# Plain block products in the first batch's first layer, a shorter range step, and the tokens' shares applied at each expert's drain

## Chip, core and metric

One core of one Trainium2 chip (trn2). The metric is the device time of one execution in microseconds (us), lower is better. TensorE (PE) multiplies, with its weight loads shown apart as PEld; VectorE (DVE), ScalarE (ACT) and GpSimd (POOL) do the elementwise work; SyncE's queue (SP) issues the transfers. PSUM holds eight banks of 128 x 512 float32 for products.

## What is computed

```python
def reference(q, k, v, centroids, w_in, w_out, w_gate, w1, w2):
    x = clustered_attention(q, k, v, centroids)   # B=2, H=8, S=768, D=64 -> x (1536, 512)
    h = x @ w_in                                  # w_in (512, 2048), held as float64
    g = np.maximum(h, 0.0) + np.log1p(np.exp(-np.abs(h)))
    x = g @ w_out                                 # MoE1; w_out (2048, 512), float64
    logits = x @ w_gate                           # (1536, 8)
    P = np.exp(logits - logits.max())
    for _ in range(8):
        P /= P.sum(1, keepdims=True) + 1e-09
        P /= P.sum(0, keepdims=True) + 1e-09
        P *= N / E
    for e in range(8):                            # MoE2: 8 experts, w1[e] (512, 1024), w2[e] (1024, 512)
        out += P[:, e:e + 1] * (np.maximum(x @ w1[e], 0.0) @ w2[e])
```

## The kernel before

Every product is taken with float32 operands split into a high and a low part, as three matmuls (high x high, high x low, low x high). The attention comes first: its steps stand in a list of events sorted by step number, and it leaves x transposed in `xt[sb]`, one tile for each of the 2 batches of 768 tokens.

The two MoE layers then run as 80 **units** (kind, batch, expert, fc): 2 x 8 units of MoE1 (kind 1) and 2 x 8 x 4 units of MoE2 (kind 2). A unit takes 256 hidden columns of one batch. Its **first layer** is `group(u, i)` (L649) for i = 0 to 6: seven block products of a Winograd-like 2 x 2 scheme, 6 matmuls of 384 columns each, 42 in all, accumulated in the PSUM banks la, lb and mb (mb shares la's or lb's bank by its tag). The scheme needs sums of blocks of x (`x_sums`, S1 to S4) and of the weights (`sums_`, T1 to T4, L215 on POOL), so the weight is split into seven slots `wh`, `wl` (L224 on ACT; L225 on POOL for kind 1, on DVE for kind 2); `w2_` splits the second weight (L230 on ACT, L231 on POOL). Banks are drained by copies c (L687) and DVE additions (L691, L695, L699), which leave the hidden values in `gf`. `act` (L706) applies softplus (Abs, Exp, Ln on ACT; a max-and-add on DVE, L720) or relu times the token's share `PB` (L727 on DVE), and `act_split` splits the result into `gh` (ACT cast, L733) and `gl` (DVE subtraction, L734). The **second layer** `layer2(u, part)` follows one unit later, in four parts between the groups of the next unit: kind 1, 24 pairs of matmuls of 512 and 256 columns (L753); kind 2, 36 matmuls of 512 columns (L772), summed over all experts in six banks y0 to y5, which are copied out at the end of a batch (L777).

`to32` (L114) turns the float64 words of w_in and w_out into float32, for batch 0's units alone (four halves of 128 x 512 a unit); batch 1 reads them back from a DRAM scratch. A half takes an Abs on ACT (L121) and on DVE a shift-and-mask (L122), two steps that join sign and low word (L123, L124) and the range step (L125), which zeroes what is too small.

In front of MoE2, `gate` and eight `sinkhorn` rounds make the shares `Pt`, from a queue of steps popped between groups. Five units (`NHOLD`) meanwhile run first layers only; then their drains (the list `late`) multiply by the shares, and their second layers follow. `spread_p` and `load_p` bring each expert's shares, spread over the partitions, from DRAM (`pb`). `GB` is the number of `gf` buffers. The program text gives a scheduler its order; each engine's instructions stand in the order that it chose.

Of the kernel before, what the change touches and what calls it, by code (L numbers as in the profile page):

```python
# [7 lines left out]
F32 = mybir.dt.float32  # L8
F32R = mybir.dt.float32r
# [11 lines left out]
def attention_moe_moe2(ctx, tc, q, k, v, centroids, w_in, w_out, w_gate, w1, w2, eye, out, dbg=None):  # L21
# [30 lines left out]
    GB = 2 * NF2 + 1  # L52
    NHOLD = 5
# [30 lines left out]

    first_blk = x_blocks(xt[0])

    def x_first(name):
        if name in SUMS:
            t = slot_pool["ap"].tile([P, KC // 2, S // 2], F32, tag="xs", name=f"xs{name}", bufs=2)
            x_sum(first_blk, name, t, nc.gpsimd)  # L90
        else:
            x_split("1_0", first_blk, int(name))

    def x_split(key, blk, i):
        name = COMBOS[i]
# [9 lines left out]
        XC[name] = hi, lo  # L105

# [7 lines left out]
    def to32(dst, raw, nm):  # L114
# [90 lines left out]
    def split_unit(u):  # L205
# [27 lines left out]
        return [sums_] + [lambda c=c: w1_(*c) for c in ((0, 2), (2, 4), (4, 7))], [lambda c=c: w2_(c) for c in range(2)]  # L233
# [383 lines left out]
    for n, x in enumerate(("S1", "S2", "3", "S4", "2", "5", "S3", "4", "0", "1", "6")):  # L617
        at(175 + n * 2, lambda x=x: x_first(x), ("xs", 0))
# [30 lines left out]
    def group(u, i):  # L649
# [54 lines left out]
    late = []  # L704

    def act(u, q, cols, ps=None):  # L706
# [4 lines left out]
        if kind == 1:  # L711
            if ps is not None:
# [25 lines left out]
    def layer2(u, part):  # L738
# [231 lines left out]
```

## Time and profile before

| | |
|---|---|
| median of 3 runs | 1684.97 us (1682.76 to 1688.23) |
| the profiled execution | 1685.95 us; span 1684.1 us |
| PE busy | 1581.2 us, 94% of the span, 8302 matmuls |
| DVE busy | 1181.9 us, 70% |
| ACT busy | 881.1 us, 52% |
| POOL busy | 776.9 us, 46% |
| granted PE clock, mean | 0.979 of full speed |

The profile is of one execution. Its span runs from the first to the last instruction; the device time has 1.85 us around it. "Busy" on DVE and POOL includes the time in which an instruction has started and is kept waiting. In a timeline each row is one instruction or a run of like ones, with its start, its length, its line, what it writes from what, its shape, how often, and in brackets the idle time of its engine before it with what ended that. Rows of a line give the shortest, the median and the longest duration in ns.

### The profile page before, as it was taken

The page shows a single profiled execution, that of the slowest core. Times are in us where ns is not written, and L with a number is a line of the kernel's source. Part 1 is how long each engine was busy: PE and PEld are TensorE (multiplying, and loading weights), DVE is VectorE, ACT ScalarE, POOL GpSimd, SP SyncE. Part 2 cuts the span into 40 slices and gives each one's busy share as a digit, 9 for nine tenths or more (in the row PEclk, how much of TensorE's full clock was granted, in tenths as well). Part 3 has the DMA queues.
Part 4 walks back from the last instruction along what each step waited for, and adds up shares of the span by engine and source line. Part 5 has one row for each costly group of instructions (what it writes and reads, how often), then busy time and mean ns, then how long its engine had stood idle before and what let it go on. Part 6 is the DMA issues. An engine that isn't in the chain of part 4 may idle for free.

```text
span 1684.1 us, 22932 instructions
## 1 busy us (share of the span) xinstructions
PE 1581.2 (94%) x8302; PEld 1404.1 (83%) x8302; DVE 1181.9 (70%) x1862; ACT 881.1 (52%) x1809; POOL 776.9 (46%) x741
## 2 busy tenths in 40 slices
PE   5899998877789998999999999999999999999999
PEld 4777887767678786889999999988999999999998
DVE  7999899899985466865655665668655555655653
ACT  5888887666667675434434433434434434433442
POOL 6444545156577665343444444445343343434441
PEclk8999999889989999999999999999999999999999
DMA  6232220044411211122122122222232122133221
GB/s 189 77 103 53 57 53 15 1 150 150 150 63 51 76 51 63 53 81 80 55 85 85 57 78 85 60 76 75 98 85 79 56 85 83 58 79 84 58 68 50
DMA packets 126017, 128.66 MB, mean 76 GB/s; under 512 B 7664, under 2 KB 99280, under 8 KB 125904
## 3 DMA queue, kind: packets, MB, share of 16 engines
q1 hardware_dynamic: 125760, 127.14, 25.2%
q8 instruction: 65, 1.06, 0.3%
q14 instruction: 48, 0.39, 0.1%
q10 hardware_dynamic: 144, 0.07, 0.0%
HBM read 107.72 MB, written 11.58 MB: 71 GB/s over the span
## 4 chain that ended last, share of the span: by engine, by line
PE 73%; DVE 17%; ACT 6%; issue 3%; POOL 1%; DMA 0%; SPq 0%; DVEq 0%; ACTq 0%
PE Y L772 30%; PE la L668 16%; PE mb L668 8%; PE lb L668 4%; PE av L571 3%; PE t L556 3%; PE s L525 3%; DVE gf L720 2%; PE y L753 2%; DVE gl L734 2%; DVE w2f L124 1%; DVE el L563 1%; DVE wl L225 1%; DVE w2f L123 1%; ACT E L538 1%
## 5 line engine op out<-in xcount | busy, mean ns | idle before, releaser
L215 POOL TENSOR_TENSOR wf<-wf 128x256 f32<-128x256 f32 x320 | 278.5, 889 | 394.2 <-DMA wf<-in_moe_w_dram 301.2
L733 ACT CAST gh<-gf 128x384 fp32r<-128x384 f32 x316 | 161.6, 513 | 490.2 <-DVE gf L727 445.5
L231 POOL TENSOR_TENSOR w2l<-w2f,w2h 128x512 fp32r<-128x512 f32 x160 | 251.5, 1592 | 320.6 <-ACT w2h L230 320.4
L772 PE MATMUL Y<-w2h,gh 128*128 128x512 f32 x768 | 299.0, 389 | 0.8 <-ACT gh L733 0.8
L772 PE MATMUL Y<-w2l,gh 128*128 128x512 f32 x768 | 298.9, 389 | 0.0
L772 PE MATMUL Y<-w2h,gl 128*128 128x512 f32 x768 | 298.5, 389 | 0.0
L734 DVE TENSOR_TENSOR gl<-gf,gh 128x384 fp32r<-128x384 f32 x316 | 224.8, 715 | 92.0 <-ACT gh L733 85.2
L695 DVE TENSOR_TENSOR gf<-la,c 128x384 f32<-128x384 f32 x79 | 43.9, 556 | 251.4 <-PE la L668 250.9
L224 ACT CAST wh<-wf 128x512 fp32r<-128x512 f32 (+1 forms) x240 | 159.2, 688 | 31.3 <-PE la L668 15.6
L772 PEld LDWEIGHTS Y<-w2h,gl 128*128 128x128 f32 x768 | 144.1, 188 | 29.9
L727 DVE SCALAR_TENSOR_TENSOR gf<-gf,pb 128x384 f32<-128x384 f32 x177 | 164.8, 932 | 4.0
L772 PEld LDWEIGHTS Y<-w2h,gh 128*128 128x128 f32 x768 | 144.0, 187 | 22.4 <-ACT gh L733 1.2
L772 PEld LDWEIGHTS Y<-w2l,gh 128*128 128x128 f32 x768 | 144.2, 188 | 21.2
L225 DVE TENSOR_TENSOR wl<-wf,wh 128x512 fp32r<-128x512 f32 (+1 forms) x195 | 150.6, 798 | 0.9 <-ACT wh L224 0.9
L668 PE MATMUL la<-chA,wh 128*128 128x384 f32 x320 | 110.7, 346 | 25.8 <-DVE gf L695 13.6
L668 PE MATMUL mb<-chS,wh 128*128 128x384 f32 x320 | 110.3, 345 | 8.9 <-DVE gf L691 8.8
L668 PE MATMUL la<-chA,wl 128*128 128x384 f32 x320 | 109.6, 342 | 3.6 <-POOL wl L225 3.6
L556 PE MATMUL t<-idf,E 128*128 128x128 f32 x576 | 100.5, 284 | 12.9 <-DVE el L563 7.3
L563 DVE TENSOR_TENSOR el<-t,eh 128x384 fp32r<-128x384 f32 x192 | 102.2, 546 | 11.9 <-ACT eh L559 9.8
L668 PE MATMUL la<-chS,wh 128*128 128x384 f32 x320 | 110.0, 344 | 0.2 <-ACT c L687 0.2
L668 PE MATMUL la<-clS,wh 128*128 128x384 f32 x320 | 109.4, 342 | 0.0
L668 PE MATMUL la<-chS,wl 128*128 128x384 f32 x320 | 109.3, 342 | 0.0
(204 smaller groups left out, 3574.6 us busy)
## 6 DMA issues: line engine op xcount, KB each, us to landing
wf<-in_moe_w_dram SPq DMA_DIRECT2D x128, 256.0 KB, 3.4
w2f<-in_moe_w_dram SPq DMA_DIRECT2D x128, 256.0 KB, 3.0
r<-in_moe_w_in_dram SPq DMA_DIRECT2D x16, 512.0 KB, 5.1
r<-in_moe_w_out_dram SPq DMA_DIRECT2D x16, 512.0 KB, 4.1
Bt<-AT SPq DMA_DIRECT2D x32, 192.0 KB, 2.5
pb<-pdram SPq DMA_DIRECT2D x15, 384.0 KB, 6.9
w<-wf SPq DMA_DIRECT2D x8, 512.0 KB, 4.3
w<-w2f SPq DMA_DIRECT2D x8, 512.0 KB, 4.2
```

Source lines behind the costliest of these rows:

```text
L215: nc.gpsimd.tensor_tensor(wf[:, SLOT[o_], :], wf[:, SLOT[u_], :], wf[:, SLOT[v_], :], ALU.subtract)
L224: nc.scalar.copy(wh[:, c0:c1], wf[:, c0 + 1 : c1 + 1, :])
L225: (nc.vector if kind == 2 or u == (1, 0, 0, 0) else nc.gpsimd).tensor_tensor(wl[:, c0:c1], wf[:, c0 + 1 : c1 + 1, :], wh[:, c0:c1].bitcast ...
L231: nc.gpsimd.tensor_tensor(w2l[:, c], w2v[:, c], w2h[:, c].bitcast(F32), ALU.subtract)
L525: nc.tensor.matmul(ps[:, kk, 0:CB], X[0, j][:, c : c + P], X[1, j][:, kk * CB : (kk + 1) * CB], start=m == 0, stop=m == 1,)
L556: nc.tensor.transpose(pt[:, t * P : (t + 1) * P], Et[i, t][:, s * P : (s + 1) * P], idf)
L563: nc.vector.tensor_tensor(el, TT.pop((i, s)), EHL[i, s].bitcast(F32), ALU.subtract)
L668: nc.tensor.matmul(ps, wt[:, s_, ks], xx[:, k_, :], start=i in (0, 1, 3) and n == 0, stop=n == 3 * nk - 1, skip_group_check=True,)
L727: nc.vector.scalar_tensor_tensor(g, src, 0.0, PB[sb, e][:, cols], ALU.max, ALU.mult)
L733: nc.scalar.copy(gh[:, cols], g)
L734: nc.vector.tensor_tensor(gl[:, cols], g, gh[:, cols].bitcast(F32), ALU.subtract)
L772: nc.tensor.matmul(y[m], gt[:, ms], wt[:, q, :], start=first and i == 0, stop=last and i == 2)
```

## The change

First, units of MoE1's first batch take plain 2 x 2 block products: `plain_group` (L703 in the changed file), four groups of 12 matmuls (48), which read the four blocks of x and of the weight themselves. Their weight has four slots, split in two pieces; the sums T1 to T4 and the x sums of that batch go, and the drains read PSUM directly. Second, `to32`'s range step becomes a maximum on the Abs result, from which the shift-and-mask then reads: on DVE two one-input and two two-input steps in place of one and three. Third, the relu of MoE2 writes `gh` (ACT) and `gl` (DVE) without the share; Y is drained after each expert by DVE as share times Y plus the sum so far (in `xt[sb]`'s memory), and `load_p`, `spread_p` and `late` go. Three units are held, with seven queue steps a unit; `gf` has 6 buffers, `gh` and `gl` 6 in place of 4.

```diff
-    GB = 2 * NF2 + 1
-    NHOLD = 5
+    GB = 6
+    NHOLD = 3
...
-        m = wp.tile([P, raw.shape[1]], F32, tag="cm", name="cm" + nm, bufs=1)
+        m = wp.tile([P, raw.shape[1]], I32, tag="cm", name="cm" + nm, bufs=1)
         d = dst.bitcast(I32)
-        nc.scalar.activation(m, H.bitcast(F32), AF.Abs)
-        nc.vector.tensor_scalar(d, H, 3, 0x3FFFFFFF, ALU.logical_shift_left, ALU.bitwise_and)
+        nc.scalar.activation(m.bitcast(F32), H.bitcast(F32), AF.Abs)
+        nc.vector.tensor_scalar(m.bitcast(F32), m.bitcast(F32), 2.0 ** -15, None, ALU.max)
+        nc.vector.tensor_scalar(d, m, 3, 0x3FFFFFFF, ALU.logical_shift_left, ALU.bitwise_and)
         nc.vector.scalar_tensor_tensor(d, H, -0x40000000, d, ALU.bitwise_and, ALU.bitwise_or)
         nc.vector.scalar_tensor_tensor(d, L, 29, d, ALU.logical_shift_right, ALU.bitwise_or)
-        nc.vector.scalar_tensor_tensor(dst, m, 2.0 ** -15, dst, ALU.is_ge, ALU.mult)
...
+        if is_plain(u):
+            return [lambda c=c: w1_(*c) for c in ((2, 4), (0, 2))], w2s
...
-    for n, x in enumerate(("S1", "S2", "3", "S4", "2", "5", "S3", "4", "0", "1", "6")):
-        at(175 + n * 2, lambda x=x: x_first(x), ("xs", 0))
+    for n in range(4):
+        at(175 + n * 5, lambda n=n: x_split("1_0", first_blk, n), ("xs", 0))
...
+    def plain_group(u, i):
...
+        q, half = i % 2, i // 2
+        ps = ps_l.tile([P, FH], F32, tag="l" + "ab"[q], name=f"p{i}" + nm)
+        nk, n = KC // 2, 0
+        for j in range(2):
+            hi, lo = XC[f"A{half + 1}{j + 1}"]
+            s_ = SLOT[f"B{j + 1}{q + 1}"]
+            for k_ in range(nk):
+                ks = slice(k_ * P, (k_ + 1) * P)
+                for wt, xx in ((wh, hi), (wh, lo), (wl, hi)):
+                    nc.tensor.matmul(ps, wt[:, s_, ks], xx[:, k_, :], start=n == 0, stop=n == 6 * nk - 1)
+                    n += 1
...
+        act(u, q, slice(half * FH, (half + 1) * FH), ps)
...
-            if ps is not None:
+            if ps is not None and not is_plain(u):
                 with tc.high_priority(40):
                     nc.scalar.copy(g, ps)
                 src = g
...
-        elif u in units[len(m1) : len(m1) + NHOLD]:
-            if ps is not None:
-                nc.scalar.copy(g, ps)
-            late.append((u, q, cols))
-            return
-        else:
-            nc.vector.scalar_tensor_tensor(g, src, 0.0, PB[sb, e][:, cols], ALU.max, ALU.mult)
-        act_split(u, q, cols)
+        else:
+            gh, gl = (t[:, cols] for t in GT[u, q])
+            nc.scalar.activation(gh, src, AF.Relu)
+            nc.vector.scalar_tensor_tensor(gl, src, 0.0, gh.bitcast(F32), ALU.max, ALU.subtract)
+            return
...
-            first, last = e == 0 and fc == 0 and part < 2, e == E - 1 and fc == FE // 2 // P - 1 and part >= 2
+            first, last = fc == 0 and part < 2, fc == FE // 2 // P - 1 and part >= 2
...
-                    o_ = mp.tile([P, DM], F32, tag="gf", name=f"out{sb}_{m}", bufs=GB)
-                    (nc.scalar.copy if m % 2 else nc.vector.tensor_copy)(o_, y[m])
+                    o_ = xt[sb].rearrange("p c s -> p (c s)")[:, m * DM : (m + 1) * DM]
+                    pr = Pt[:, sb * NT + m, e : e + 1]
+                    if e == 0:
+                        nc.vector.tensor_scalar(o_, y[m], pr, None, ALU.mult)
+                    else:
+                        nc.vector.scalar_tensor_tensor(o_, y[m], pr, o_, ALU.mult, ALU.add)
...
-                queue += [lambda: load_p(0, 0), spread_p]
-            k = 4 if held == 0 else 5
+            k = 7
```

The first place is DVE in MoE1's first batch, where unit 4 is drained while unit 5's weights are converted (`r` is the float64 weight, `cm` the Abs result, `w2f` and `wf` the float32 weights, `u` the softplus' logarithm, `p` a plain group's bank). Before:

```order
L122 TENSOR_SCALAR w2f_0_5_5218<-r_0_5_5220 128x512
L720 SCALAR_TENSOR_TENSOR gf_0_4_5236<-gf_0_4_5236,u_0_4_00_5252 128x384
L125 SCALAR_TENSOR_TENSOR wf_0_5_5217<-cm_10_0_5_5285,wf_0_5_5217 128x512
L123 SCALAR_TENSOR_TENSOR w2f_0_5_5218<-r_0_5_5220,w2f_0_5_5218 128x512
L734 TENSOR_TENSOR gl_0_4_5238<-gf_0_4_5236,gh_0_4_5237 128x384
```

After:

```order
L737 SCALAR_TENSOR_TENSOR gf_0_4_5179<-p_0_4_5166,u_0_4_00_5182 128x384
L121 TENSOR_SCALAR w2f_0_5_5155<-cm_10_0_5_5279 128x512
L122 SCALAR_TENSOR_TENSOR w2f_0_5_5155<-r_0_5_5157,w2f_0_5_5155 128x512
L745 TENSOR_TENSOR gl_0_4_5181<-gf_0_4_5179,gh_0_4_5180 128x384
L123 SCALAR_TENSOR_TENSOR w2f_0_5_5155<-r_0_5_5157,w2f_0_5_5155 128x512
L120 TENSOR_SCALAR cm_10_0_6_5369<-cm_10_0_6_5369 128x512
```

The drain of the hidden values now reads a bank, the conversion reads `cm` at its second step, and no instruction of L125's kind is left.

The second place is DVE at a change of expert in MoE2 (batch 0, from expert 2's last unit to expert 3's first). Before:

```order
L727 SCALAR_TENSOR_TENSOR gf_3_0_9108<-gf_3_0_9108,pb_9086 128x384
L734 TENSOR_TENSOR gl_3_0_9110<-gf_3_0_9108,gh_3_0_9109 128x384
L727 SCALAR_TENSOR_TENSOR gf_3_0_9105<-la_3_0_9098,pb_9086 128x384
L225 TENSOR_TENSOR wl_3_2_9228<-wf_3_2_9220,wh_3_2_9226 128x512 x2
L734 TENSOR_TENSOR gl_3_0_9107<-gf_3_0_9105,gh_3_0_9106 128x384
```

After:

```order
L741 SCALAR_TENSOR_TENSOR gl_3_0_8967<-gf_3_0_8965,gh_3_0_8966 128x384
L793 SCALAR_TENSOR_TENSOR x_69<-Y_2_0_8594,Pt,x_69 128x512
L741 SCALAR_TENSOR_TENSOR gl_3_0_8967<-gf_3_0_8965,gh_3_0_8966 128x384
L793 SCALAR_TENSOR_TENSOR x_69<-Y_2_1_8595,Pt,x_69 128x512
L793 SCALAR_TENSOR_TENSOR x_69<-Y_2_2_8596,Pt,x_69 128x512
L225 TENSOR_TENSOR wl_3_2_9087<-wf_3_2_9079,wh_3_2_9085 128x512
L741 SCALAR_TENSOR_TENSOR gl_3_0_8964<-la_3_0_8955,gh_3_0_8963 128x384
```

Three drains of expert 2's Y stand ahead of the drain that frees la; three more follow behind it.

The third place is PE at the end of the hold (`cp` is a round's sum over the tokens, Y_0 the first expert's second layer). Before, the last `cp` and what follows it:

```order
L835 MATMUL cp_7867<-cs_7823,ones_f 128x8
L668 MATMUL mb_1_0_7910<-chS_0_7251,wh_1_0_7733 128x384
L668 MATMUL mb_1_0_7910<-clS_0_7252,wh_1_0_7733 128x384
L668 MATMUL mb_1_0_7910<-chS_0_7251,wl_1_0_7735 128x384
L668 MATMUL mb_1_0_7910<-chS_0_7251,wh_1_0_7733 128x384
L668 MATMUL mb_1_0_7910<-clS_0_7252,wh_1_0_7733 128x384
L668 MATMUL mb_1_0_7910<-chS_0_7251,wl_1_0_7735 128x384
L668 MATMUL la_1_0_7853<-chA_0_7269,wh_1_0_7733 128x384
L668 MATMUL la_1_0_7853<-clA_0_7270,wh_1_0_7733 128x384
L854 MATMUL pb_0_7885<-idf,Pt 128x128 x3
L854 MATMUL pb_1_7890<-idf,Pt 128x128 x3
L843 MATMUL ptT<-idf,Pt 96x128
```

After, two of the rounds' sums:

```order
L850 MATMUL cp_7554<-cs_7544,ones_f 128x8
L783 MATMUL Y_0_2_7689<-w2h_0_0_7050,gl_0_0_7305 128x512
L783 MATMUL Y_0_3_7690<-w2h_0_0_7050,gh_0_0_7304 128x512
L783 MATMUL Y_0_3_7690<-w2l_0_0_7052,gh_0_0_7304 128x512
L783 MATMUL Y_0_3_7690<-w2h_0_0_7050,gl_0_0_7305 128x512
L783 MATMUL Y_0_4_7691<-w2h_0_0_7050,gh_0_0_7304 128x512
L783 MATMUL Y_0_4_7691<-w2l_0_0_7052,gh_0_0_7304 128x512
L783 MATMUL Y_0_4_7691<-w2h_0_0_7050,gl_0_0_7305 128x512
L783 MATMUL Y_0_0_7687<-w2h_0_1_7293,gh_0_1_7451 128x512
L783 MATMUL Y_0_0_7687<-w2l_0_1_7295,gh_0_1_7451 128x512
L850 MATMUL cp_7609<-cs_7593,ones_f 128x8
```

Before, a second layer's first matmul stood 28 rows behind the last of the eight sums; now it stands ahead of the third, and the last four sums lie among second layers as here.

## Rows read from the trace of the kernel before

**Rows 1.** The page: the span and each engine's busy time.
```profile
span 1684.1 us, 22932 instructions
PE 1581.2 (94%) x8302; PEld 1404.1 (83%) x8302; DVE 1181.9 (70%) x1862; ACT 881.1 (52%) x1809; POOL 776.9 (46%) x741
```
**Rows 2.** Stretch, length, PE, PEld, DVE, ACT, POOL busy (count), clock, DMA, GB/s.
```profile
0.00:327.20 327.20, 284.65 (x1794) 243.45 (x1794) 291.42 (x566) 251.48 (x575) 150.28 (x208) 0.96 0.25 70
327.20:515.90 188.70, 148.23 (x721) 129.95 (x722) 175.96 (x215) 120.11 (x242) 120.62 (x85) 0.90 0.35 117
515.90:659.70 143.80, 135.51 (x744) 118.94 (x743) 89.83 (x107) 101.68 (x212) 89.16 (x70) 1.00 0.20 63
659.70:749.80 90.10, 86.33 (x432) 72.20 (x431) 63.19 (x144) 36.91 (x73) 34.77 (x34) 1.00 0.20 60
749.80:1684.10 934.30, 926.48 (x4617) 839.53 (x4616) 561.51 (x831) 370.92 (x710) 382.02 (x346) 1.00 0.25 74
```
**Rows 3.** PE's timeline at unit starts of MoE1, both batches.
```profile
342.99 0.69 PE L668 MATMUL la<-chA,wl 128*128 128x384 f32 x1 [2.58 <-POOL wl L225]
...
479.27 0.69 PE L668 MATMUL la<-chA,wh 128*128 128x384 f32 x1 [5.17 <-DVE gf L695]
...
515.19 0.51 PE L753 MATMUL y<-gl,w2h 128*128 128x512 f32 x2
515.54 0.51 PE L753 MATMUL y<-gh,w2l 128*128 128x512 f32 x2
515.89 0.33 PE L668 MATMUL la<-chA,wh 128*128 128x384 f32 x1
516.06 0.34 PE L668 MATMUL la<-clA,wh 128*128 128x384 f32 x1
```
**Rows 4.** Lines from 343 to 479 us: count, shortest/median/longest ns, first and last start.
```profile
L122 DVE TENSOR_SCALAR wf<-r x12: 413/424/1528, 351.3 to 461.1; 128x512 int32<-128x512 int32 x12
L123 DVE SCALAR_TENSOR_TENSOR w2f<-r,w2f x13: 673/1214/2308, 345.0 to 473.8; 128x512 int32<-128x512 int32 x13
L720 DVE SCALAR_TENSOR_TENSOR gf<-gf,u x23: 543/547/1649, 346.2 to 467.5; 128x384 f32<-128x384 f32 x23
L734 DVE TENSOR_TENSOR gl<-gf,gh x24: 543/551/1651, 341.7 to 470.1; 128x384 fp32r<-128x384 f32 x24
L695 DVE TENSOR_TENSOR gf<-la,c x6: 541/543/550, 356.9 to 478.7; 128x384 f32<-128x384 f32 x6
L215 POOL TENSOR_TENSOR wf<-wf x24: 732/993/3547, 357.1 to 473.4; 128x256 f32<-128x256 f32 x24
L225 POOL TENSOR_TENSOR wl<-wf,wh x20: 1299/1721/2297, 342.9 to 476.0; 128x512 fp32r<-128x512 f32 x13, 128x768 fp32r<-128x768 f32 x7
L231 POOL TENSOR_TENSOR w2l<-w2f,w2h x12: 1288/1613/1872, 348.7 to 464.2; 128x512 fp32r<-128x512 f32 x12
```
**Rows 5.** Timelines of DVE, POOL and ACT late in the attention.
```profile
289.10 7.41 DVE L545 TENSOR_SCALAR sc<-sc 128x3 f32<-128x3 f32 x1
...
292.77 3.56 POOL L104 TENSOR_TENSOR clA<-x,chA 128x768 fp32r<-128x768 f32 x2
...
297.26 0.90 ACT L538 ACTIVATE E<-s,sc 128x768 f32<-128x768 f32 x1 [7.19 <-DVE sc L533]
```
**Rows 6.** PE's timeline in the hold: two successive rounds' sums over the tokens.
```profile
703.63 0.39 PE L835 MATMUL cp<-cs,ones_f 128*128 128x8 f32 x2 [1.01 <-DVE cs L831]
...
707.88 0.39 PE L835 MATMUL cp<-cs,ones_f 128*128 128x8 f32 x2
```
**Rows 7.** Where a MoE2 unit hands over: PE's and DVE's timelines, and the page's cast.
```profile
883.67 0.34 PE L668 MATMUL la<-chA,wl 128*128 128x384 f32 x1
883.85 0.39 PE L772 MATMUL Y<-w2h,gh 128*128 128x512 f32 x1
884.08 0.39 PE L772 MATMUL Y<-w2l,gh 128*128 128x512 f32 x1
...
885.89 0.34 PE L668 MATMUL la<-chA,wh 128*128 128x384 f32 x1
...
884.91 0.55 DVE L727 SCALAR_TENSOR_TENSOR gf<-la,pb 128x384 f32<-128x384 f32 x1
...
L733 ACT CAST gh<-gf 128x384 fp32r<-128x384 f32 x316 | 161.6, 513 | 490.2 <-DVE gf L727 445.5
```

More of the change, by code (lines that the diff above doesn't have):

```diff
@@ L105, in x_split, with is_plain @@
         XC[name] = hi, lo
+    def is_plain(u):
+        return u[:2] == (1, 0)
     SLOT = {"B12": 0, "B22": 1, "B11": 2, "B21": 3, "T1": 4, "T2": 5, "T3": 6, "T4": 7}
@@ L231, in w2_ @@
             nc.gpsimd.tensor_tensor(w2l[:, c], w2v[:, c], w2h[:, c].bitcast(F32), ALU.subtract)
-        return [sums_] + [lambda c=c: w1_(*c) for c in ((0, 2), (2, 4), (4, 7))], [lambda c=c: w2_(c) for c in range(2)]
+        w2s = [lambda c=c: w2_(c) for c in range(2)]
+        if is_plain(u):
+            return [lambda c=c: w1_(*c) for c in ((2, 4), (0, 2))], w2s
+        return [sums_] + [lambda c=c: w1_(*c) for c in ((0, 2), (2, 4), (4, 7))], w2s
     att = ExitStack()
@@ L673, in group @@
         if i == 0:
-            if u == units[len(m1) + 4]:
-                t = wp.tile([P, 2, S], F32, tag="raw", name="gfx", bufs=2)
-                GF[u, 0], GF[u, 1] = t[:, 0], t[:, 1]
             for q in range(2):
-                if (u, q) not in GF:
-                    GF[u, q] = mp.tile([P, S], F32, tag="gf", name=f"gf{q}" + nm, bufs=GB)
+                GF[u, q] = mp.tile([P, S], F32, tag="gf", name=f"gf{q}" + nm, bufs=GB)
                 GT[u, q] = tuple(
-                    mp.tile([P, S], F32R, tag=t, name=f"{t}{q}" + nm, bufs=4) for t in ("gh", "gl")
+                    mp.tile([P, S], F32R, tag=t, name=f"{t}{q}" + nm, bufs=2 * NHOLD) for t in ("gh", "gl")
                 )
@@ L702, in group @@
             act(u, 0, be, ps)
-    late = []
+    def plain_group(u, i):
+        nm = f"{u[0]}{u[1]}_{u[2]}_{u[3]}"
+        wh, wl = W[u][:2]
+        q, half = i % 2, i // 2
[9 more added lines that the diff above has]
+                    n += 1
+        if half == 0:
+            GF[u, q] = mp.tile([P, S], F32, tag="gf", name=f"gf{q}" + nm, bufs=GB)
+            GT[u, q] = tuple(mp.tile([P, S], F32R, tag=t, name=f"{t}{q}" + nm, bufs=2 * NHOLD) for t in ("gh", "gl"))
+        act(u, q, slice(half * FH, (half + 1) * FH), ps)
     def act(u, q, cols, ps=None):
@@ L764, in layer2 @@
         else:
-            first, last = e == 0 and fc == 0 and part < 2, e == E - 1 and fc == FE // 2 // P - 1 and part >= 2
+            first, last = fc == 0 and part < 2, fc == FE // 2 // P - 1 and part >= 2
             if first and r == 0:
-                Y[2, sb] = [ps_y.tile([P, DM], F32, tag=f"y{m}", name=f"Y{sb}_{m}") for m in range(6)]
+                Y[2, sb] = [ps_y.tile([P, DM], F32, tag=f"y{m}", name=f"Y{sb}_{e}_{m}") for m in range(6)]
             y = Y[2, sb]
@@ L886, in attention_moe_moe2 @@
                 queue += [lambda it=it, ph=ph: sinkhorn(it, ph) for it in range(8) for ph in range(2)]
-                queue += [lambda: load_p(0, 0), spread_p]
-            k = 4 if held == 0 else 5
+            k = 7
             extra, queue = queue[:k], queue[k:]
-        if kind == 2 and fc == 0 and not hold:
-            load_p(sb, e)
         if n + 2 in starts:
@@ L904, in attention_moe_moe2 @@
         for i in range(7):
-            group(u, i)
+            if not is_plain(u):
+                group(u, i)
+            elif i % 2 == 0:
+                plain_group(u, i // 2)
             run(steps.get(i, []))
             if n + 1 in starts:
-                x_split(f"{units[n + 1][0]}_{units[n + 1][1]}", sums, i)
+                key = f"{units[n + 1][0]}_{units[n + 1][1]}"
+                if not is_plain(u):
+                    x_split(key, sums, i)
+                else:
+                    for c in ((4,), (5,), (0, 1), (), (), (), (2, 3, 6))[i]:
+                        x_split(key, sums, c)
             if extra:
@@ L928, in attention_moe_moe2 @@
             run(queue)
-            for lu, q, cols in late:
-                if (0, lu[2]) not in PB:
-                    load_p(0, lu[2])
-                g = GF[lu, q][:, cols]
-                nc.vector.scalar_tensor_tensor(g, g, 0.0, PB[0, lu[2]][:, cols], ALU.max, ALU.mult)
-                act_split(lu, q, cols)
             while len(pend) > 1:
```

52 lines of the change are left out of this document (11 added, 41 removed).

## The prediction

> **What bounds the kernel now.** I read the page first: PE is busy for 1581 of 1684 us [rows 1], so at most some 100 us of idle PE can go without a cut in its work, and the change adds work: 48 matmuls in place of 42 in eight units. Next the table by stretches [rows 2], which shows where those 100 us lie. In MoE2 (749.8 to 1684.1) PE idles 8 us of 934, in MoE1's second batch 8 of 144, in the hold (659.7 to 749.8) 4 of 90, in MoE1's first batch 40 of 189, in the attention 43 of 327. The first batch also has the lowest granted clock, 0.90: part of its busy PE runs at 1.2 GHz in place of 2.4. There DVE is "busy" for 176 us and POOL for 121, 297 together in 189. So that stage is the one to look into, then the hold, whose 90.1 us I compare with its work, then the hand-over of a MoE2 unit, where the new drains must fit.
>
> In the first batch the timeline gives a pitch of (479.27 - 342.99)/6 = 22.7 us a unit, and its unit starts wait for DVE and POOL [rows 3]. The rows by line say why [rows 4]. DVE's two-input steps on SBUF take 0.54 to 0.67 us at best but up to 1.65 and 2.31, POOL's operations are spread likewise, while L695, which reads a bank as one input, never leaves 0.54 to 0.55. So an SBUF operation of DVE and one of POOL exclude each other, and what reads PSUM does not take part. Then the times of the two engines add up. At their shortest, one unit before has: conversion 4 x (0.41 + 3 x 0.67) = 9.7; L720 and L734, 8 x 0.54 = 4.3; three bank additions 1.6; POOL 4 x 0.73 + 2 x 1.30 + one of 768 columns at 1.5 x 1.30 + 2 x 1.29 = 10.1. The sum, 25.7, is 1.13 times the pitch, as it should be if successive instructions of one engine overlap a little. So DVE and POOL together bound this stage.
>
> **First part: plain products and the shorter range step.** A unit now has conversion 4 x (2 x 0.41 + 2 x 0.67) = 8.6, the subtraction 4 x 0.54 = 2.2 and POOL 2 x 1.30 + 2 x 1.29 = 5.2 in the shared time: 16.0. The four softplus drains read a bank, 2.2, beside POOL's work or not. Divided by 1.13 this is 14.2 without and 16.1 with them. PE becomes the later one: a group's matmul steps by 0.17, a pair by 0.35 [rows 3], so 48 x 0.17 + 24 x 0.35 = 16.6 us at full clock. At this stage's present 0.90 it would be 18.4. I take 18.2, since PE will be denser but the units still wait for Abs, range step and a load in turn; floor 16.6, ceiling 20.5. Six pitches give 6 x (18.2 - 22.7) = -27. The first unit, 15.8 us before (327.2 to 342.99), needs two weight pieces in place of three and 8.2 us of matmuls: I take 12, -4. From 479.27 to 515.9, 36.6 us, stand the last unit and two second layers, at full clock 8.2 + 2 x 8.4 = 25; I take 30, -6.5. Together **-37.5**, bounds -25 and -46. Loads must keep up: the DMA share of 0.35 [rows 2] becomes 0.44, far from full.
>
> The order rows on DVE bear one risk: each conversion now begins with a step that needs ACT's Abs, where L122 could start before. ACT is busy for 120 of 189 us [rows 2] and loses three bank copies and four casts' worth of slots, so I cost it at nothing in the sum and put it into a rival.
>
> In the attention POOL makes the split of x in one dense run. In its midst a DVE step of three columns takes 7.41 us, until POOL's last subtraction ends at 292.77 + 3.56 = 296.33, and ACT's exponent waits 7.19 for it [rows 5]. The change takes away the four sums and three of seven splits and spreads the rest over steps of five. I take **-5**; bounds 0 (a new stall at another place) and -7.3. The Trainium skill, SBUF — State Buffer, section "SBUF: two separate sides", says that the port pair of DVE and GpSimd is a lock held for one instruction, so the loser waits until that instruction ends. By that rule the stall would be one subtraction, 1.8, and the sum 1644 in place of 1641. The row shows a wait across all that was queued on POOL, so I go by the row.
>
> A rule speaks against bank-reading drains: the Trainium skill, Perfetto Trace Analysis, section "Optimizing Scalar/DVE Operations", gives DVE about 60 ns of access on SBUF and 125 on PSUM. By it four drains in eight units would cost 2 us more, 1643. L695 with its bank and L734 without have the same shortest time, 0.54 [rows 4], so here the trace does not agree.
>
> MoE1's second batch keeps its work; six `gf` buffers now serve four x sums and the drains, which can hold up a transition or ease it: **0**, bounds -3 and +5.
>
> **Second part: shares at the drain, three units held.** The hold has five units' groups and four second layers: 5 x 42 x 0.17 + 4 x 36 x 0.23 = 69 us ([rows 3, 7] for the steps), and takes 90.1. The other 21 are the gate, stalls and late drains. The rounds are a chain of 4.25 us each (703.63 to 707.88) [rows 6], 34 in all, before covered by groups alone. Now three units' groups (21), the gate (some 6, an estimate from the excess) and two second layers (17) cover the chain as the order rows of PE show. The last four sums lie nine or ten Y matmuls apart, 2.1 to 2.3 us, less than a round, so some 4 to 6 us of waiting remain. Two ordinary units then follow, and the same work ends in about 81: **-9**, bounds -2 and -12.
>
> A MoE2 unit's hand-over: la's last matmul ends at 884.01, nine Y matmuls later, at 885.89, la is written again, and DVE freed it at 884.91 + 0.55 = 885.46 [rows 7]. The new drain is a Relu on ACT (a cast takes 0.51) and then a DVE step of 0.55: with two short hand-overs of 0.1, 885.3, so a regular unit loses nothing. Its cover is 0.6 us of Y matmuls; without it the Relu's whole time would show. At each change of expert DVE gets six more drains. One of 512 columns takes an estimated 0.54 x 512/384 = 0.73, and three stand ahead of the drain that frees la. Filling idle DVE (busy 562 of 934 us [rows 2]) they cost nothing; all three in the way cost 2.2 - 0.4 = 1.8. I take 0.5, since y's banks finish one after the other and the first drains start early: 15 changes give **+7**, bounds 0 and +27. The transfers of `pb`, the late multiplications and the spread leave SP, DVE and PE, but none ended a wait of the regular units: 0. At the end six drains take the place of six copies of which ACT did half: +0.1.
>
> **Sum.** -5 - 37.5 + 0 - 9 + 7 = -44.5, against the profiled execution's 1685.95: **1641** us. The three runs' median, 1684.97, lies 1 us below it.
>
> **The rivals.** *B, the first batch stays coupled.* Conversion waits for Abs, the second layer starts with the half that is drained last, and a unit takes 20.7 in place of 18.2. For it: the unit starts already wait on both DVE and POOL [rows 3]. Against it: 10 us less in the shared time. Then the six pitches give -12, the first unit -4, the end -4, in all -20; with -5 - 9 + 7 the time is 1658. *C, slower: la is freed too late in every MoE2 unit.* The drain needs ACT and then DVE. If the Relu stands behind two weight casts on ACT and the DVE step behind a weight subtraction (L225), the chain from la's last matmul is some 3.1 us against the 1.88 available, 1.2 us a unit, and 62 units lose 74: 1641 + 74 - 7 = 1708. It decides from 51.5/62 = 0.83 us a unit, where nothing of the gain is left. For it: the hand-over has 0.4 us left now [rows 7]. Against it: ACT is busy for 371 of 934 us, and a wait of DVE between the multiplication and POOL goes. *D, PE alone bounds the first batch and the boundaries cost nothing:* -46 - 12 - 7 = -65, 1621. That the change doesn't do what it says is excluded by the order rows: the range step, the sums and the share's multiplications are gone.
>
> **Numbers.** Forecast 0.62, own range 1630 to 1652; B 0.17; D 0.11; C 0.10. About 0.3%, 5 us, is what a measurement of this kernel can tell from no change. Forecast, B and D are faster by more: 0.90. C is split: 0.06 slower, 0.04 where it just eats the gain. The range, 1620 to 1665, takes in D and B and leaves out C and the far bounds.
>
> **What would show it.** Right: in the first batch a pitch near 18, a stage near 151 us, a granted clock above 0.90, and unit starts that wait for no POOL operation; no seven-microsecond DVE step in the attention; sums over tokens among Y matmuls and some 81 us for the hold's work; MoE2 units at 15.6 us with waits on la only at changes of expert. Wrong: POOL and DVE still stretched with PE idle at each unit (B), or PE waiting on la for the step that writes `gl` in every MoE2 unit (C).

## Result: 22 us faster, half of what was forecast

The changed kernel takes 1663.4 us (median of 4 runs, 1659.88 to 1669.19), the kernel before 1685.96 (4 runs): ratio 0.987, 95% interval 0.984 to 0.990. The profiled execution took 1662.58, span 1660.8. The measured time lies above the forecast's own range, 1630 to 1652. The page and the table by stretches of the changed kernel (columns as in [rows 2]; the stretches end where a stage's first matmul stands, 31.1 us of ordinary units are cut out to compare the hold):

```profile
span 1660.8 us, 22729 instructions
PE 1581.5 (95%) x8337; PEld 1405.6 (85%) x8337; DVE 986.6 (59%) x1669; ACT 865.3 (52%) x1757; POOL 660.5 (40%) x692
```

```profile
0.00:314.10 314.10, 278.46 (x1794) 236.40 (x1794) 279.97 (x567) 251.75 (x575) 130.35 (x194) 0.99 0.27 73
314.10:480.80 166.70, 147.73 (x768) 133.53 (x769) 124.69 (x189) 103.58 (x202) 71.25 (x54) 0.94 0.42 136
480.80:627.80 147.00, 138.30 (x744) 121.67 (x743) 89.25 (x107) 101.81 (x212) 87.71 (x69) 0.98 0.18 58
627.80:684.30 56.50, 52.45 (x241) 41.07 (x240) 32.74 (x99) 20.05 (x39) 15.51 (x18) 0.94 0.13 38
684.30:715.40 31.10, 31.10 (x157) 28.10 (x156) 13.33 (x22) 12.35 (x24) 8.42 (x9) 1.00 0.23 68
715.40:1660.80 945.40, 933.45 (x4640) 844.84 (x4638) 446.63 (x687) 375.73 (x709) 347.29 (x350) 0.99 0.22 68
```

Against [rows 2]: the attention is 13.1 us shorter (forecast 5), MoE1's first batch 22.0 (forecast 37.5), its second batch 3.2 longer (forecast 0). From the first held unit to the second group of MoE2's seventh unit, which both kernels reach with the same groups and second layers done, PE's timeline gives 102.4 us before and 104.2 after: 1.9 longer where 9 shorter was forecast. The rest of MoE2 is 6.6 longer (forecast 7), but elsewhere than forecast. -13.1 - 22.0 + 3.2 + 1.9 + 6.6 = -23.4, the difference of the two spans (23.3) but for rounding.

In MoE1's first batch PE's starts of the second layer's first part show a pitch of (436.20 - 353.49)/4 = 20.7 us (from the second unit's first matmul to the eighth's it is 123.4 us, 20.6 a unit), with a wait for `gl` in each unit. PE's timeline:

```profile
353.49 0.61 PE L764 MATMUL y<-gl,w2h 128*128 128x512 f32 x2 [2.10 <-DVE gl L745]
...
374.15 0.62 PE L764 MATMUL y<-gl,w2h 128*128 128x512 f32 x2 [0.88 <-DVE gl L745]
...
394.63 0.62 PE L764 MATMUL y<-gl,w2h 128*128 128x512 f32 x2 [1.58 <-DVE gl L745]
...
414.94 0.61 PE L764 MATMUL y<-gl,w2h 128*128 128x512 f32 x2 [3.15 <-DVE gl L745]
...
436.20 0.94 PE L764 MATMUL y<-gl,w2h 128*128 128x512 f32 x2 [0.86 <-DVE gl L745]
```

What stands ahead of `gl` at 394: POOL's splits of two weights in one burst, and on DVE a conversion step that waits for the burst's end. POOL's and DVE's timelines:

```profile
388.60 2.56 POOL L225 TENSOR_TENSOR wl<-wf,wh 128x512 fp32r<-128x512 f32 x2 [13.36 <-ACT wh L224]
391.09 2.55 POOL L231 TENSOR_TENSOR w2l<-w2f,w2h 128x512 fp32r<-128x512 f32 x2
```

```profile
390.87 0.56 DVE L737 SCALAR_TENSOR_TENSOR gf<-p,u 128x384 f32<-128x384 f32 x1 [3.10 <-ACT u L736]
393.68 0.43 DVE L121 TENSOR_SCALAR w2f<-cm 128x512 int32<-128x512 int32 x1 [2.26 <-POOL w2l L231]
394.02 0.55 DVE L745 TENSOR_TENSOR gl<-gf,gh 128x384 fp32r<-128x384 f32 x1
```

POOL has had nothing to do for 13 us here and then works for 5 at the change of unit, when the second layer needs its first drains.

### The profile page after: what moved, and what is told of

It is laid out like the page before. It is cut to its first block, busy times and chain, and to the rows that moved or that the text cites. A ratio compares the mean times of both kernels' runs of the same rounds, so it can differ in the third digit from the quotient of the medians.

```text
span 1660.8 us, 22729 instructions
## 1 busy us (share of the span) xinstructions
PE 1581.5 (95%) x8337; PEld 1405.6 (85%) x8337; DVE 986.6 (59%) x1669; ACT 865.3 (52%) x1757; POOL 660.5 (40%) x692
## 4 chain that ended last, share of the span: by engine, by line
PE 76%; DVE 11%; ACT 6%; POOL 3%; DMA 2%; issue 2%; SPq 0%; DVEq 0%; POOLq 0%; ACTq 0%
PE Y L783 30%; PE la L671 16%; PE mb L671 8%; PE y L764 4%; PE lb L671 4%; PE av L574 3%; PE t L559 3%; PE s L528 2%; PE p L716 2%; DVE el L566 1%; DVE gf L737 1%; DVE gl L745 1%; DVE wl L225 1%; DVE sc L536 1%; POOL wf L213 1%
## 5 line engine op out<-in xcount | busy, mean ns | idle before, releaser
L213 POOL TENSOR_TENSOR wf<-wf 128x256 f32<-128x256 f32 x288 | 223.3, 797 | 375.9 <-DMA wf<-in_moe_w_dram 331.3
L231 POOL TENSOR_TENSOR w2l<-w2f,w2h 128x512 fp32r<-128x512 f32 x160 | 225.2, 1428 | 347.9 <-ACT w2h L230 341.1
L740 ACT ACTIVATE gh<-gf 128x384 fp32r<-128x384 f32 x192 | 100.9, 525 | 301.9 <-DVE gf L694 194.8
L225 DVE TENSOR_TENSOR wl<-wf,wh 128x512 fp32r<-128x512 f32 (+1 forms) x194 | 166.8, 880 | 72.3 <-ACT wh L224 71.5
L741 DVE SCALAR_TENSOR_TENSOR gl<-gf,gh 128x384 fp32r<-128x384 f32 x192 | 123.9, 650 | 32.0 <-ACT gh L740 29.3
L686 ACT COPY c<-la 128x384 f32<-128x384 f32 x144 | 69.0, 479 | 116.6 <-PE la L671 116.2
L230 ACT CAST w2h<-w2f 128x512 fp32r<-128x512 f32 x160 | 92.4, 618 | 44.2 <-PE Y L783 18.5
L562 ACT CAST eh<-t 128x384 fp32r<-128x384 f32 x192 | 92.2, 482 | 26.0 <-PE t L559 14.4
L671 PE MATMUL la<-chA,wh 128*128 128x384 f32 x288 | 98.3, 341 | 3.5 <-DVE gl L741 3.5
L671 PE MATMUL mb<-chS,wl 128*128 128x384 f32 x288 | 98.4, 342 | 0.0
```

Source lines behind the costliest of these rows:

```text
L213: nc.gpsimd.tensor_tensor(wf[:, SLOT[o_], :], wf[:, SLOT[u_], :], wf[:, SLOT[v_], :], ALU.subtract)
L230: nc.scalar.copy(w2h[:, c], w2v[:, c])
L231: nc.gpsimd.tensor_tensor(w2l[:, c], w2v[:, c], w2h[:, c].bitcast(F32), ALU.subtract)
L562: nc.scalar.copy(eh, TT[i, s])
L671: nc.tensor.matmul(ps, wt[:, s_, ks], xx[:, k_, :], start=i in (0, 1, 3) and n == 0, stop=n == 3 * nk - 1, skip_group_check=True,)
L740: nc.scalar.activation(gh, src, AF.Relu)
```

## Experiments

All are the changed kernel with the edit shown, but for the range step alone, which starts from the kernel before. Ratios are against the kernel before on the same chip. Stage lengths are read from PE's timeline, from the first matmul of one stage to that of the next; each comes from one profile, and a few us of a stage are within what it shows here without an edit of its own: MoE1's second batch took 143 to 148 us over these runs.

| run | median us | ratio, 95% | first batch | first held to first ordinary unit | change of batch |
|---|---|---|---|---|---|
| changed kernel | 1663.4 | 0.987 [0.984, 0.990] | 166.7 | 56.5 | 122.6 |
| e1 drain order | 1659.8 | 0.985 [0.983, 0.987] | 162.8 | 56.0 | 120.7 |
| e2 sums in idle buffers | 1653.7 | 0.982 [0.980, 0.984] | 166.7 | 56.0 | 117.3 |
| e3 range step alone | 1682.5 | 0.998 [0.997, 1.000] | see below | as before | 116.3 |
| e4 dense splits | 1663.3 | 0.987 [0.985, 0.989] | 166.4 | 56.3 | 122.8 |
| e5 two w2f buffers | 1667.7 | 0.989 [0.986, 0.993] | 170.3 | 55.6 | 122.7 |
| e6 late split | 1656.5 | 0.982 [0.979, 0.984] | 167.5 | 51.5 | 122.9 |
| e7 four edits | 1648.0 | 0.978 [0.975, 0.980] | 162.3 | 51.6 | 115.7 |
| e8 old range step | 1665.7 | 0.988 [0.985, 0.990] | 170.4 | 56.6 | 123.0 |
| e9 two Abs buffers | 1659.1 | 0.985 [0.982, 0.988] | 166.9 | 56.5 | 120.7 |
| e10 splits on DVE | 1645.5 | 0.975 [0.973, 0.978] | 153.4 | 55.9 | 121.8 |
| e11 e9 and e10 | 1643.1 | 0.974 [0.972, 0.975] | 148.4 | 56.0 | 123.5 |
| e12 e2, e6, e9, e10 | 1635.9 | 0.970 [0.968, 0.972] | 148.7 | 51.8 | 117.9 |

("Change of batch": seven unit pitches across it, 116.0 in the kernel before.)

**MoE1's first batch.** First the order of the drains:

```diff
-        q, half = i % 2, i // 2
+        q, half = 1 - i // 2, i % 2
```

> The changed kernel with one edit: a plain unit computes both halves of the tokens of its second 256-column half of the hidden values (q = 1) in its first two groups and q = 0 in its last two, so that the half with which the second layer begins is no longer the one that is drained last. Theory: the 2.3 us of idle PE in each unit of MoE1's first batch (waits on gl and gh at the first part of the second layer) come from that order; they go, and with them most of the low clock: pitch from 20.7 to about 17.5 us, the stage from 166.7 to about 150, the time about 15 us below the changed kernel (1663 to about 1648). Rival: the conversion on DVE and POOL sets the pitch (a step of it that waits for the single w2f buffer stands ahead of gl in DVE's queue); then the same idle time shows up at another wait, the pitch stays above 20 and the time within 4 us of 1663.

The last unit's groups of the first half here multiply blocks of the next batch, so this kernel computes another output; the order of the work is otherwise the one named. The waits on `gl` and `gh` are gone from the list of PE's waits, but nearly as much stands at the next place, the bank that waits for its drain. PE's waits in the stage (us in total, times, longest), changed kernel and e1:

```profile
PE y L764 <- DVE gl L745: 9.0, 6, 3.2
PE p L716 <- DVE gf L737: 6.9, 4, 3.1
PE y L764 <- ACT gh L744: 2.8, 3, 1.9
PE p L716 <- ACT wh L224: 1.3, 1, 1.3
```

```profile
PE p L716 <- DVE gf L737: 16.6, 8, 5.2
PE p L716 <- ACT wh L224: 1.8, 1, 1.8
PE p L716 <- DVE wl L225: 1.4, 1, 1.4
```

So the order mostly chooses where PE waits; the rival held in the time, 3.6 us below, while the pitch came out just under its 20 (19.9 by the units' first matmuls). Next, the buffer, with one wf tile kept for all plain units:

```diff
+        if is_plain(u) and fc % 2:
+            w2f = wf[:, 4:8, :].rearrange("p s f -> p (s f)")
```

> The changed kernel with one edit: every second unit of MoE1's first batch converts its w_out words into the half of the wf tile that plain products leave free, so that there are two buffers for w2f and not one. Theory (from the run with the drains in another order, where the idle time only moved): a conversion step that waits some 2.3 us for w2f, until POOL has split the unit before, stands ahead of the drains in DVE's queue, and each unit of MoE1's first batch loses that time twice, as idle PE and as low clock. With two buffers the step no longer waits: pitch from 20.7 to 17.5 to 18.5 us, the stage from 166.7 to 150 to 155, the time about 12 below 1663. Rival: conversion as a whole sets the pitch (loads, Abs, one buffer for cm); then the idle time of DVE moves to another step, the stage stays above 162 and the time within 4 us of 1663.

The stage got no shorter, 170.3. DVE's wait for POOL's split is gone, and the same steps now run beside POOL's burst and are stretched, with `gl` the longest. POOL's, DVE's and PE's timelines of e5:

```profile
413.52 2.69 POOL L238 TENSOR_TENSOR w2l<-wf,w2h 128x512 fp32r<-128x512 f32 x2 [0.31 <-ACT w2h L237]
...
415.12 1.65 DVE L122 SCALAR_TENSOR_TENSOR wf<-r,wf 128x512 int32<-128x512 int32 x1
416.70 2.16 DVE L752 TENSOR_TENSOR gl<-gf,gh 128x384 fp32r<-128x384 f32 x1
...
418.91 0.62 PE L771 MATMUL y<-gl,w2h 128*128 128x512 f32 x2 [3.32 <-DVE gl L752]
```

That left POOL's burst itself, and ACT's wait for the one Abs buffer, which also showed in the timelines. Two edits, apart and together:

```diff
-        m = wp.tile([P, raw.shape[1]], I32, tag="cm", name="cm" + nm, bufs=1)
+        k_ = RAW["cm"] = 1 - RAW.get("cm", 1)
+        m = RAW["wf"][:, 4 + 2 * k_ : 6 + 2 * k_, :].rearrange("p s f -> p (s f)").bitcast(I32)
```

> The changed kernel with one edit: the Abs results of the conversion alternate between two places in the part of the wf tile that plain products leave free, in place of the one buffer cm. Theory: since the range step reads Abs first, ACT's Abs of the next half waits up to 3 us for DVE to have read cm, and in ACT's queue the logarithm of a softplus stands behind it; DVE's drain, and PE's bank, wait for that logarithm. With two places this wait goes: the stage falls from 166.7 to 152 to 158 and the time to about 1652. Rival: DVE and POOL still exclude each other, and POOL's burst of four splits at the end of a unit (5 to 6 us with DVE's steps stretched to 1.6) sets the idle time; then the stage stays within 4 us of 166.7.

```diff
-            (nc.vector if kind == 2 or u == (1, 0, 0, 0) else nc.gpsimd).tensor_tensor(
+            (nc.vector if kind == 2 or is_plain(u) else nc.gpsimd).tensor_tensor(
...
-            nc.gpsimd.tensor_tensor(w2l[:, c], w2v[:, c], w2h[:, c].bitcast(F32), ALU.subtract)
+            (nc.vector if is_plain(u) else nc.gpsimd).tensor_tensor(w2l[:, c], w2v[:, c], w2h[:, c].bitcast(F32), ALU.subtract)
```

> The changed kernel with one edit: in MoE1's first batch both weight splits (wl and w2l, 4 operations of 512 columns a unit) run on DVE in place of POOL. Theory of the exclusion: DVE's steps are no longer stretched, a unit's 16.0 us of shared time become 10.8 + 4 x 0.67 = 13.5, and the stage falls from 166.7 to 152 to 158. Rival, the one buffer cm and the order on ACT: the stage stays within 4 us of 166.7, or is longer by what DVE has to do in addition (8 x 2.7 = 21 at most).

> The changed kernel with both edits, two places for Abs and the splits on DVE. If the two causes both cost, the stage comes near PE's 134 us of matmuls plus its ends, 143 to 150, and the time to about 1645. If one of them is the whole of it, the result is that of the better single edit. If neither is, and the stage's low clock or the ends of the stage (first unit, last two second layers) hold the time, it stays above 160.

Two Abs buffers alone changed nothing in the stage (166.9), the splits on DVE took 13.3 us off it, and with them the Abs buffers gave 5 more (148.7 again in e12; 2.4 us in the medians), as e10's theory and e11's first case had it. The stretch of the first batch in e10 and e11, with a granted clock of 0.98 and 0.99 in place of 0.94:

```profile
313.50:466.90 153.40, 141.51 (x768) 128.03 (x769) 122.91 (x219) 103.59 (x202) 29.41 (x24) 0.98 0.45 148
```

```profile
314.90:463.30 148.40, 140.05 (x768) 126.42 (x769) 121.92 (x218) 102.09 (x201) 28.52 (x24) 0.99 0.47 153
```

DVE is busy for no longer than in the changed kernel (122.9 against 124.7 us) though it has 30 operations more. One of them takes 0.68 us on DVE where POOL takes 1.3, so an estimated 30 x 0.68 = 20 us of DVE's busy time in the changed kernel was time kept waiting. The rows of L231 in the stage, changed kernel and e10:

```profile
L231 POOL TENSOR_TENSOR w2l<-w2f,w2h x12: 1262/1297/1722, 328.9 to 435.7; 128x512 fp32r<-128x512 f32 x12
```

```profile
L231 DVE TENSOR_TENSOR w2l<-w2f,w2h x13: 679/683/1980, 333.3 to 444.1; 128x512 fp32r<-128x512 f32 x13
```

The Trainium skill, Perfetto Trace Analysis, section "Optimizing Scalar/DVE Operations", warns that GpSimd and DVE share an SBUF port, so that moving work between the two might not help. The trace agrees that this work was not free for DVE while it stood on POOL: DVE was busy for 124.7 us then and for 122.9 with the work its own. Moving it back took 13.3 us off the stage.

PE's waits in the changed kernel name no POOL operation, so the splits cost PE's time through DVE and ACT. e10 takes away two things at once, DVE's wait for the splits and the stretch of its steps beside them. e5 took the wait alone and gained nothing; no run takes the stretch alone.

**The range step**, alone on the kernel before and undone in the changed one:

```diff
-        nc.vector.tensor_scalar(d, H, 3, 0x3FFFFFFF, ALU.logical_shift_left, ALU.bitwise_and)
+        nc.vector.tensor_scalar(m.bitcast(F32), m.bitcast(F32), 2.0 ** -15, None, ALU.max)
+        nc.vector.tensor_scalar(d, m, 3, 0x3FFFFFFF, ALU.logical_shift_left, ALU.bitwise_and)
```

> The kernel before with only the new range step (maximum on the Abs result, one two-input step fewer a half). Theory: it takes the six conversion steps out of DVE's first 17 us (they wait for Abs now), so that the attention runs 4 to 5 us ahead from 40 us on; the stall of 7 us at 289 us stays, MoE1's first batch gains some 8 us of its 189 (DVE's and POOL's shared time falls from 25.7 to 24.6, and 1.1 us over seven units is 7). Time about 1674, 12 below before. Rival: the lead at the start is a chance of the one profile; then the attention ends at 327 as before and the time is about 1678.

> The changed kernel with the old range step (one one-input and three two-input steps a half). Theory: in the changed kernel DVE is idle for some 40 us of the 167 of MoE1's first batch, but conversion lies on the path there (it waits for w2f, then the drains wait for it), and four times 0.26 us a unit more make the stage 4 to 8 us longer: 1667 to 1671. Rival: the steps fill DVE's idle time; stage and time within 2 us of the changed kernel's.

Alone it gained 0.2%, 3 us, a quarter of the expectation; MoE1's two batches together took 331.6 us against 332.5. (In e3 groups of the second batch start among the first batch's last second layers, so the stage has no length of its own.) From the second unit's first matmul to the eighth's its first batch took 136.7 us against 145.4, about the gain expected, but the rest of MoE1 was 8.8 us longer, each by one profile; why stays open. The attention ended at 328.9, so the rival was right that the range step brings no lead there. Undone in the changed kernel it cost 3.7 us of the stage, by one profile and within the spread named above, and 2.3 us in the medians, which their intervals don't tell from nothing.

**The attention.**

```diff
-        at(175 + n * 5, lambda n=n: x_split("1_0", first_blk, n), ("xs", 0))
+        at(175 + n * 1, lambda n=n: x_split("1_0", first_blk, n), ("xs", 0))
```

> The changed kernel with one edit: the four splits of x for the first unit follow each other closely (one step of the event list apart, not five), eight operations of POOL in some 10 us. Theory: a step of DVE that meets such a run waits for all of it, 5 to 10 us, ACT and PE wait for that step, and PE's clock falls after it: the attention ends 7 to 13 us later than 314 and the time is 1670 to 1676. Rival, one instruction as the most that DVE waits: the attention ends at most 2 us later, 1663 to 1665.

This edit tested neither side: POOL's four splits stand in one run of 10 us in the changed kernel too (270.65 to 281.07), whatever steps they are given. What e3 shows is that the long stall comes with the old work of POOL, since it stands there unchanged. DVE's timelines of e3 and of the changed kernel:

```profile
291.24 7.42 DVE L545 TENSOR_SCALAR sc<-sc 128x3 f32<-128x3 f32 x1
```

```profile
277.33 0.16 DVE L548 TENSOR_SCALAR sc<-sc 128x3 f32<-128x3 f32 x1
```

Over that stretch (from PE's 331st to its 337th av matmul: 14.1 us before, 5.3 after) the changed kernel is 8.8 us ahead. The other 4 us of the attention's 13 were there before 60 us and went with the granted clock, 0.81 from 24 to 60 us before and 0.96 in the changed kernel. They are not shown to be the change's: e1 has the changed kernel's attention, and there it ended at 318.3, not 314.2. (Over twelve runs with that attention the 331st av matmul starts between 284.0 and 288.4 us; before it was 288.6, in e3 290.7, so a small part may be the change's.) The stretch from 24 to 60 us in the changed kernel and in e1:

```profile
24.00:60.00 36.00, 30.36 (x195) 26.91 (x193) 29.13 (x60) 28.32 (x66) 16.05 (x23) 0.96 0.34 96
```

```profile
24.00:60.00 36.00, 31.19 (x173) 28.26 (x174) 25.95 (x53) 24.33 (x57) 12.81 (x19) 0.82 0.33 91
```

**The hold.** In the changed kernel PE waits for the fifth round's sum, and DVE, just before, waits for ACT to start a weight split of expert 1's first unit, which the scheduler put between the round's steps. In the edit `LB["sk"]` is a round's last step on DVE. PE's and DVE's timelines:

```profile
668.83 0.60 PE L850 MATMUL cp<-cs,ones_f 128*128 128x8 f32 x2 [2.57 <-DVE cs L846]
```

```profile
667.30 0.96 DVE L225 TENSOR_TENSOR wl<-wf,wh 128x768 fp32r<-128x768 f32 x1 [2.17 <-ACT wh L224]
```

```diff
+        LB["sk"] = nc.cur_bb.bb.instructions[-1]
...
+            if held == NHOLD:
+                def behind(fn):
+                    with tc.issue_after(LB["sk"]):
+                        fn()
+                c = [lambda fn=fn: behind(fn) for fn in c]
```

> The changed kernel with one edit: the weight split of expert 1's first unit is put behind the last round of the gate's normalisation on DVE. Theory: in the hold, one of those splits waits 2.2 us for ACT and POOL with a step of the fifth round behind it; PE idles 2.6 us on the round's sum and its clock falls to 0.85 for the second layers. Without it no round takes longer than 4.5 us, the 56.5 us from the first held unit to the first ordinary one become 51 to 53, and the time falls by 4 us to about 1659. Rival: the chain is bound by its own steps and by the sums' places among the Y matmuls; then the stretch stays within 1.5 us of 56.5.

It held: 56.5 became 51.5, and e7 and e12 repeat it. Only the first three rounds still took 5.7 to 6.2 us, not 4.5 at most, with PE busy with first layers between their sums. The stretch of the second layers in the changed kernel and in e6 (e6's row takes in six matmuls of the next unit; up to that unit it is 18.3 us, for the matmuls that took 23.3):

```profile
661.00:684.30 23.30, 20.69 (x81) 16.43 (x81) 11.66 (x41) 3.61 (x7) 8.93 (x10) 0.85 0.11 33
```

```profile
662.80:682.00 19.20, 19.06 (x86) 14.82 (x86) 11.35 (x41) 3.52 (x6) 5.50 (x6) 1.00 0.14 43
```

**The change of batch.**

```diff
-        for name in SUMS:
-            t = slot_pool["mp"].tile([P, KC // 2, S // 2], F32, tag="gf", name=f"x{name}{key}", bufs=GB)
+        for n, name in enumerate(SUMS):
+            if key == "1_1":
+                t = slot_pool["mp"].tile([P, KC // 2, S // 2], F32, tag="gf", name=f"x{name}{key}", bufs=GB)
+            else:
+                if n % 2 == 0:
+                    two = wp.tile([P, 2, KC // 2, S // 2], F32, tag="raw", name=f"x{name}{key}", bufs=2)
+                t = two[:, n % 2]
```

> The changed kernel with one edit: the four sums of x for MoE2's two batches are kept in the two buffers of the float64 weights, idle by then, and not in four of the six gf buffers. Theory: the change of batch inside MoE2 takes 6.6 us more than before (six units in 91.4 us against 84.8) because only two gf buffers are left to the drains there; it goes back to about 85, and the time falls by about 6 us (1663 to 1657); the end of MoE1 may give 1 to 3 more. Rival: the longer transition comes from the drains of Y and the order around them; then it stays near 91 and the time within 2 us.

It held: 5.3 of the 6.6 us came back. The wait that goes is the largest of PE's there; the list from 1090 to 1183 us in the changed kernel, and in e2:

```profile
PE la L671 <- DVE gl L741: 3.5, 1, 3.5
PE la L671 <- ACT c L686: 2.9, 1, 2.9
PE mb L671 <- DVE gf L690: 1.8, 1, 1.8
```

```profile
PE la L676 <- ACT c L691: 2.9, 1, 2.9
PE mb L676 <- DVE gf L695: 1.8, 1, 1.8
```

**Together.**

> The changed kernel with four edits together: two w2f buffers, the second layer's first half drained first in all plain units but the last, the sums of x for MoE2 in the idle float64 buffers, the late split. If the three losses are separate they add: 12 to 15 from MoE1's first batch, 6 to 9 from the change of batch, 4 from the hold: 1636 to 1642. If they share a cause (a clock that falls for other reasons), about 1650.

The hold and the change of batch added as expected; the first batch, with e1's and e5's edits, did not (162.3), and the time stayed 6 us above the range. With e9's and e10's edits in their place:

> The changed kernel with the edits that each took away one loss: splits of MoE1's first batch on DVE, two places for its Abs results, the sums of x for MoE2 in the idle float64 buffers, the late split behind the gate's rounds. If the losses are separate, their gains add: 20 (the two edits of the first batch together), 5 to 7 (change of batch and the end of MoE1) and 5 (hold), 1663 - 31 = 1632, range 1628 to 1637. If they overlap, 1638 to 1643.

1635.9 us, by the medians 27.5 below the changed kernel and 50 below the one before (ratio 0.970, 0.968 to 0.972), inside the expected range. This is the best version found.

## Why the prediction was off, step by step

- **The pitch of MoE1's first batch.** That DVE and POOL bind this stage together was read rightly (e10). The step that failed is "PE becomes the later one ... I take 18.2". Measured was 20.6. First, its scale was wrong. The two rows of [rows 3] that give the pitch are not unit starts: 342.99 lies inside the second unit's first group, and 479.27 is the seventh unit's last group. The second and the eighth unit start here, in PE's timeline before:

```profile
339.61 0.44 PE L668 MATMUL la<-chA,wh 128*128 128x384 f32 x1 [2.67 <-ACT wh L224]
...
485.01 0.34 PE L668 MATMUL la<-chA,wh 128*128 128x384 f32 x1
```

  So the pitch before was 145.4/6 = 24.2, not 22.7, and the sum of 25.7 takes in 1.6 of bank additions that by its own reading take no part. 24.1 against 24.2 leaves no factor of 1.13: the new unit's shared time is 16.0 to 18.2, on either side of PE's 16.6. Second, that sum was compared with PE's time as if it were spread evenly over the unit. A third of it, POOL's four splits, comes as one burst at the change of unit, where `gl` stands in DVE's queue behind a step that either waits for the burst (changed kernel) or is stretched by it (e5). With the burst moved to DVE the pitch was 19.3 us (e10).
- **The wait for Abs**, put at nothing in the sum, costs nothing beside the burst (e9) and 5 us of the stage once the burst is gone: with both edits (e11) the pitch was 18.4, near the forecast's 18.2, and the stage 148.4, near its 151.
- **The ends of that stage.** By the units' first matmuls the first unit went from 12.4 to 14.6 us (forecast from 15.8 to 12), the last unit with its two second layers from 30.9 to 28.7 (forecast from 36.6 to 30). The 10.5 us forecast there did not come; 9.1 of them belonged to the misread pitch.
- **Rival B** gave the pitch, 20.7, and 1658 us (its terms make 1659), both close, but that is in part luck. Of its reasons, the order of the halves (e1) and the wait for Abs (e9) are each worth 4 us or nothing as long as the burst is there.
- **The attention**, -5 forecast: the stall went with all it carried, 8.8 us, since PE's clock had fallen after it (0.88 before, 1.00 after, from 270 to 314 us). That the splits would be spread over steps of five was wrong.
- **The hold**, -9 forecast, +1.9 measured. The failed step is "the same work ends in about 81": the 21 us of excess were taken as cover that the second layers would fill. But PE was busy for 86.3 of those 90.1 us [rows 2]. Only the 3.8 of idle PE and 1.8 of matmuls for `pb` and `ptT` could go. And 4 of the 21 were ordinary work: the stretch to 749.8 also holds two groups of the sixth unit and nine Y matmuls of the fifth. The chain of a round was also mis-sized at 4.25: 21 matmuls of first layers fill the time between the two sums of [rows 6], and among second layers in e6 a round took 2.6 us. What the change added is a wait: the prediction counted Y matmuls between the sums, not what else stands in DVE's queue between a round's steps. The splits of one unit there cost 5 us (e6).
- **The expert changes**, +7 forecast, cost nothing: three units with a change among them keep the pitch of 15.58. The first lb matmul of each, and the six drains of Y, which fit into idle DVE (0.74 us each where 0.73 was estimated):

```profile
763.27 0.34 PE L671 MATMUL lb<-chA,wh 128*128 128x384 f32 x1
...
778.85 0.34 PE L671 MATMUL lb<-chA,wh 128*128 128x384 f32 x1
...
794.42 0.34 PE L671 MATMUL lb<-chA,wh 128*128 128x384 f32 x1
```

```profile
773.86 0.74 DVE L793 SCALAR_TENSOR_TENSOR x<-Y,Pt,x 128x512 f32<-128x512 f32 x1
774.99 1.39 DVE L793 SCALAR_TENSOR_TENSOR x<-Y,Pt,x 128x512 f32<-128x512 f32 x2
...
777.50 2.06 DVE L793 SCALAR_TENSOR_TENSOR x<-Y,Pt,x 128x512 f32<-128x512 f32 x3
```

- In their place came the loss at the change of batch: of the six `gf` buffers four went to sums. The prediction named these buffers, for MoE1's second batch alone, and gave them no price in MoE2. That +7 was forecast for the rest of MoE2 and 6.6 measured is luck.
- **Rival C** fell: regular units hand over without a wait (PE has none in the list from 732 to 1090 us). The Relu in place of a multiplication costs MoE2 nothing.
- The 3.2 us of MoE1's second batch are not explained; e9 to e12 have 143 to 145.5 there with the same code.

## What to carry to other kernels

Where two engines exclude each other, don't add their times to a mean and compare it with PE's: look where in the unit the other engine's work falls, and what stands behind it in an in-order queue at that moment. An operation that is twice as fast on the contended engine (0.68 against 1.3 us here) can be cheaper there than off it. When a chain is hidden behind matmuls, read the whole queue of the engine that carries the chain, not only PE's order, and when buffers are cut, price them at every change of stage.

## What was not expected of the hardware

- A wait of PE costs more than its length. In the hold PE waited 2.57 us and the stretch's granted clock was 0.85; without the wait (e6) it was 1.00 and the same matmuls took 18.3 us in place of 23.3. In MoE1's first batch the clock rose from 0.94 to 0.98 (e10) and 0.99 (e11) as waits went.
- The same attention, in the same order, ends between 313.5 and 318.3 us in twelve runs; the granted clock from 24 to 60 us was 0.96 where it ended at 314.2 and 0.82 where it ended at 318.3.
- A DVE step of three columns again took 7.42 us in another execution (e3), with POOL's operations back to back. Why one such step is caught across several of them and others are not stays open.
- The drain that reads a bank beside one SBUF input (L737) took 0.54 to 0.56 us in all 24 cases between 330 and 450 us of the changed kernel, with POOL's burst beside some of them (390.87 above).
